# Two linear-attention and two MLP layers on one core: layer-norm statistics of the next layer's first four row tiles, dealt to two engines and issued later

## The chip, the core and the metric

The kernel runs on one core of one Trainium2 chip. A core has five engines, each with an instruction queue of its own that is worked in order: TensorE (PE in the profile; its weight loads are PEld), VectorE (DVE), ScalarE (ACT), GpSimd (POOL) and SyncE (SP), which issues the DMAs here. TensorE writes its results to PSUM, from where VectorE and ScalarE fetch them. The metric is the device time of one execution in microseconds (us).

## What is computed

x has 2048 rows of 576 features, in bfloat16. Four layers follow one another: attention, MLP, attention, MLP, with the same weights in both rounds. Cut to what matters:

```
def _layernorm(x): return (x - mean(x)) / sqrt(var(x) + 1e-5)

def A(x):                                    # 32 heads of 18
    q, k, v = split(x @ wqkv)
    phi = lambda t: where(t > 0, t + 1, exp(t)) + 1e-6
    kv  = sum over rows of phi(k)^T v        # per head
    z   = sum over rows of phi(k)
    return (phi(q) @ kv) / (phi(q) . z + 1e-6)  @ wo

def B(x):                                    # F = 4608
    y = _layernorm(x)
    return gelu(y @ w1 + b1) @ w2 + b2

x = x + A(_layernorm(x)); x = x + B(_layernorm(x))
x = x + A(_layernorm(x)); x = x + B(_layernorm(x))
```

B normalizes its already normalized input once more; the kernel does both at once, with one variance and a changed epsilon.

## The kernel before, in words

Rows are worked in 16 row tiles of 128 and in 4 chunks of 4 row tiles. An attention layer (`layer_A`, li = 0 and li = 2) first makes keys and values and their sums over all rows, and then, in its output stage, goes through the row tiles t = 0 to 15 (the loop at L827). The MLP layer that follows (`LayerB`) needs the first chunk, row tiles 0 to 3, normalized and transposed in `yT` before its first matmul; the other chunks it loads and normalizes later, beside its own matmuls.

**The output stage, one pass t.** `wo_stage(t)` (L787) multiplies the scaled features `pq` with `kvwo` (ten matmuls of 288 columns, L792, into one of two PSUM tiles, `accA` and `accB` in turns) and calls `residual`, where VectorE adds the old row and writes the new one (L515); SyncE stores it to `x_d` (L522). Then come the query projections that are left (`q_proj`, L585, whose features ScalarE makes with L464 and L465 and VectorE with L472 and L476), and the scaling of the next chunk: `den_stage(c)` (L746) makes the denominators of chunk c on TensorE (L754) and their reciprocals on ScalarE as exp(-ln) (L758, L761; the name of the last is kept in `act_last["rden"]`); `quad_stage` (L767) spreads them on VectorE; `scale_stage(g, c)` (L775), five times a chunk, broadcasts them over the head rows by a 512-column matmul (L780), ScalarE copies the result out of PSUM (L782), and VectorE multiplies `pq` by it (L783). Passes 0, 4 and 8 hold three broadcasts, passes 1, 5 and 9 two and behind them the denominators of the chunk after next. The broadcasts, the denominators, the query projections and the transposes below share four PSUM buffers (`ps_h`, tag h).

**The layer norm of a row tile** goes through `LNPipe`. `feed` adds an item, and each `tick` moves every item by one step; a pass of the output stage has two ticks up to t = 9 and one from then on. An item's `hold` counts ticks that it lets pass. The steps: statistics; `ln_rstd` on GpSimd (L372); `ln_nmr` on GpSimd (L376); the normalized row into one of three `y_ring` tiles on GpSimd (L389, with a small copy, L399); the transposes on TensorE (L421), not before pass `tp_at`; and their copy into `yT` on ScalarE (L428). Statistics there are in two kinds. With `stats="act"` ScalarE goes over the row twice, for the mean (L333, Identity with an accumulated sum) and in the next tick for the squares (L340), and GpSimd makes the variance (L342). With `stats="dve"` VectorE does two `bn_stats` (L349, L350), a `bn_aggr` (L356) and a scalar step (L366); if the item has `after`, the two `bn_stats` are ordered behind the instruction that `after` names, for "sum" the last residual sum issued so far.

**What sets the order.** The program's order is a wish: a scheduler puts each engine's instructions in order when they are ready by its own reckoning, earlier issued ones first. TensorE's order in these stages is fixed by a chain (`pe`). `add_manual_dep(..., NOSYNC, ...)` adds an edge of order between two instructions of one engine's queue, without a semaphore.

**Rows.** The new rows, the old rows that are loaded ahead (four tiles, `prefetch_xo`) and the pairs of old rows of the first layer share a ring of nine buffers (`rows`, tag row). A row of tiles 0 to 3 is held until it is stored and normalized.

Of the kernel before, what the change touches and what calls it, by code (L numbers as in the profile page):

```python
# [7 lines left out]
ACT = mybir.ActivationFunctionType  # L8
# [6 lines left out]
S, D, F, H, DH = 2048, 576, 4608, 32, 18  # L15
# [19 lines left out]
def build(tc, A_x, A_wqkv, A_wo, B_w1, B_b1, B_w2, B_b2, out, dbg=None, n_layers=4):  # L35
    nc = tc.nc
    dbg = dbg or {}
    with ExitStack() as ctx:
# [80 lines left out]
        def row_tile(name):  # L119
            return rows.tile([P, D], F32, name=name, tag="row")  # L120
# [3 lines left out]
        NOSYNC = mybir.DependencyInfo(mybir.DependencyClass.NoSync, mybir.DependencyReason.SCHED_ONLY)  # L124
# [13 lines left out]
        def pe(inst):  # L138
            if pe_chain["on"]:
                if pe_chain["last"] is not None:  # L140
                    tc.add_manual_dep(inst.ins, pe_chain["last"], NOSYNC, reason="TensorE order in the MLP")
                pe_chain["last"] = inst.ins.name
            return inst
# [157 lines left out]
        class LNPipe:  # L301
# [11 lines left out]
            def tick(self, transposes=1):  # L313
                land()
                for it in list(self.items):
# [8 lines left out]
                    if st == -1:  # L324
                        xn = row_tile("xl")
# [4 lines left out]
                    elif st == 0 and it["stats"] == "act":  # L330
                        mv = it["mv"] = work.tile([P, 2], F32, name="ln_mv", bufs=6)
                        it["dump"] = blk.tile([P, D], BF16, name="ln_dump", tag="blk")
                        nc.scalar.activation(out=it["dump"][:], in_=it["xt"][:, 0:D], func=ACT.Identity,  # L333
                                             scale=-1.0 / D, accum_out=mv[:, 0:1])
                        it["stage"] = 0.5
                        continue
                    elif st == 0.5:
                        u = it["u"] = work.tile([P, 1], F32, name="ln_u", bufs=4)
                        mv = it["mv"]
# [6 lines left out]
                    elif st == 0:  # L346
                        xt = it["xt"]
                        stt = work.tile([P, 2, 6], F32, name="ln_st", bufs=4)
                        first = nc.vector.bn_stats(out=stt[:, 0, :], in_=xt[:, 0:HALF])  # L349
                        second = nc.vector.bn_stats(out=stt[:, 1, :], in_=xt[:, HALF:D])  # L350
                        after = dve_last["sum"] if it["after"] == "sum" else it["after"]
# [3 lines left out]
                        mv = work.tile([P, 2], F32, name="ln_mv", bufs=6)  # L355
# [23 lines left out]
                    elif st in (2, 3):  # L379
# [4 lines left out]
                        xt = it["xt"]  # L384
                        if it["norm"] == "act":
                            nc.scalar.activation(out=y[:, 0:D], in_=xt[:, 0:D], func=ACT.Identity,
                                                 scale=it["rstd"][:, 0:1], bias=it["nmr"][:, 0:1])
# [18 lines left out]
                    elif st == 4:  # L406
                        y = it["y"]
                        t = it["t"]
# [6 lines left out]
                        first = it["kind"] == "A" and t < 2  # L415
# [26 lines left out]
        lnp = LNPipe()  # L442
        act_last = dict(exp=None, gelu=None)
# [57 lines left out]
        def residual(li, t, halves):  # L501
            xo = xo_of.pop((li, t))
            last = (li == n_layers - 1)
            if last:
                xn = rows.tile([P, 2 * D], BF16, name="xbf", tag="row")[:, 0:D]
            elif li == 0:
                xn = row_tile("xn")[:]
            else:
                xn = xo
            parts = [slice(h * HALF, (h + 1) * HALF) for h in range(2)] if last and t == NT - 1 else [slice(0, D)]  # L510
            for i, cols in enumerate(parts):
                if len(parts) == 2:
                    total = nc.vector.tensor_tensor(out=xn[:, cols], in0=halves[i][:, 0:HALF], in1=xo[:, cols], op=ALU.add)
                else:
                    total = nc.vector.tensor_tensor(out=xn[:, cols].rearrange("p (h n) -> p h n", h=2), in0=halves,  # L515
                                                    in1=xo[:, cols].rearrange("p (h n) -> p h n", h=2), op=ALU.add)
                dve_last["sum"] = total.ins.name
                if last:
                    nc.sync.dma_start(out=out_f[t * P:(t + 1) * P, cols], in_=xn[:, cols])
            if last:  # L520
                return None
            nc.sync.dma_start(out=x_d[t], in_=xn)  # L522
            return xn

        def layer_A(li, next_kind, pre_a1=None):
# [261 lines left out]
            def wo_stage(t):  # L787
                c, j = divmod(t, TPC)
                wp = ps_acc.tile([P, 2, 512], F32, name="wo_ps", tag=("accA", "accB")[t % 2])
                for half in range(2):  # L790
                    for g in range(G):
                        pe(nc.tensor.matmul(wp[:, half, 0:HALF], lhsT=pq[(g, c)][0:GR[g], j * P:(j + 1) * P],  # L792
                                              rhs=kvwo[g][0:GR[g], half * HALF:(half + 1) * HALF],
                                              start=(g == 0), stop=(g == G - 1)))
                xn = residual(li, t, wp[:, :, 0:HALF])
                if xn is not None and next_kind == "B" and t < TPC:
                    lnp.feed(xn, t, "B", "pool", "act", hold=1, stats="act", tp_at=6 + 2 * t)

            for t in range(AHEAD):
                prefetch_xo(li, t, add_b2=False)  # L800
# [26 lines left out]
            for t in range(NT):  # L827
                c, j = divmod(t, TPC)
                if t + AHEAD < NT:
                    prefetch_xo(li, t + AHEAD, add_b2=False)  # L830
                wo_stage(t)
                for late in list(rden_of):
                    quad_stage(late, after=dve_last["sum"])
                if q_left:
                    q_proj(*q_left.pop(0))
                if c + 1 < NCA:
                    for g in ((0, 1, 2), (3, 4), (), ())[j]:
                        scale_stage(g, c + 1)
                if j == 1 and c + 2 < NCA:
                    den_stage(c + 2)  # L840
                if t == NT - 3:
                    warm_table(ACT.Gelu_apprx_tanh, act_last["copy"])
                state["wo"] = t
                lnp.tick()
                if t < 10:
                    lnp.tick(transposes=0)
# [237 lines left out]
```

## Time and profile before

| | |
|---|---|
| median of 3 runs | 768.49 us (768.37 to 768.53) |
| the profiled execution, its own time | 768.48 us |
| its span, from the first instruction to the last | 766.7 us |
| TensorE busy | 760.5 us (99%) |
| ScalarE busy | 341.5 us (45%) |
| VectorE busy | 269.5 us (35%) |
| GpSimd busy | 123.9 us (16%) |
| output stage of the first attention layer | about 78 to 107 us |
| output stage of the second | about 454 to 482 us |

Times in the views are microseconds from the start of the span. A timeline row has start, length, engine, line, operation, out<-in with the program's tile names, shapes and count; in brackets the idle time of the engine before it and who ended it. A row of groups has busy time and the mean of one in ns. Matmuls overlap one another, so a busy TensorE is not one at its pace: that is read from the starts. The line numbers are those of the code above.

### The profile page before, as it was taken

The numbers are of one execution on the slowest core, as the hardware profiler recorded it, in microseconds if no ns is written. First come the engines' busy times: TensorE is split into PE (matmuls) and PEld (weight loads), VectorE is DVE, ScalarE is ACT, GpSimd is POOL, SyncE is SP. The second block draws the span as 40 slices with busy tenths as digits, with TensorE's granted clock in tenths as the row PEclk, the third lists the DMA queues.
The fourth block names the chain that finished last, engine by engine and source line by source line (L and its number), as shares of the span: only waits on it lengthen the run. The fifth ranks groups of instructions, "written<-read, shape, count | busy, mean of one in ns | idle before, by whom it ended". The sixth has DMA issues, their size and how long they took to land.

```text
span 766.7 us, 15671 instructions
## 1 busy us (share of the span) xinstructions
PE 760.5 (99%) x6522; PEld 492.6 (64%) x6522; DVE 269.5 (35%) x669; ACT 341.5 (45%) x768; POOL 123.9 (16%) x202
## 2 busy tenths in 40 slices
PE   9999999999999999999999999999999999999998
PEld 6776664675477457646777767447745764674476
DVE  7786764035113603400455677600140032000000
ACT  5888956304710660164056578560065027205600
POOL 4681412012100301200110004300020011001000
PEclk9999999999999999999999999999999999999999
DMA  9992483016402721330246007530131033011000
GB/s 262 264 302 48 140 276 79 28 57 164 123 24 62 194 70 40 96 87 1 73 122 214 1 16 247 203 81 15 51 107 50 17 124 81 9 32 55 2 9 24
DMA packets 80289, 73.82 MB, mean 96 GB/s; under 512 B 36698, under 2 KB 64858, under 8 KB 80218
## 3 DMA queue, kind: packets, MB, share of 16 engines
q1 hardware_dynamic: 80218, 72.82, 32.3%
q8 instruction: 51, 0.84, 0.5%
q14 instruction: 20, 0.16, 0.1%
HBM read 48.03 MB, written 24.77 MB: 95 GB/s over the span
## 4 chain that ended last, share of the span: by engine, by line
PE 96%; ACT 3%; DVE 1%; issue 0%; DMA 0%; ACTq 0%
PE m_ps L965 36%; PE h_ps L907 20%; PE hp_ps L907 16%; PE q_ps L585 5%; PE wo_ps L792 3%; PE k_ps L537 3%; PE k_ps L608 3%; PE k_ps L625 2%; PE v_ps L558 1%; PE m_half L965 1%; PE v_ps L555 1%; ACT rden_bc L782 1%; PE tp L421 1%; ACT ln_dump L333 1%; PE kvacc L579 1%; PE k_tail L625 1%
## 5 line engine op out<-in xcount | busy, mean ns | idle before, releaser
L965 PE MATMUL m_ps<-w_sb,hT 128*128 128x288 bf16 x2232 | 274.8, 286 | 0.0
L965 PEld LDWEIGHTS <-hT 128*128 128x128 bf16 x2304 | 224.8, 98 | 59.8 <-issue 3.4
L907 PEld LDWEIGHTS <-w_sb 64*128 64x128 bf16 x2304 | 124.5, 94 | 136.4 <-issue 1.9
L907 PE MATMUL hp_ps<-yT,w_sb 64*128 64x512 bf16 x1152 | 178.0, 376 | 0.0
L907 PE MATMUL h_ps<-yT,w_sb 64*128 64x512 bf16 x1152 | 147.9, 376 | 0.0
L912 ACT COPY relay_sb<-relay_sb 128x1 f32<-128x1 f32 x144 | 28.6, 198 | 262.9 <-PE h_ps L907 220.0
L903 ACT ACTIVATE hT<-h_ps,b1T 128x512 bf16<-128x512 f32 x144 | 91.2, 684 | 43.8 <-PE h_ps L907 43.8
L372 POOL TENSOR_TENSOR ln_rstd<-ln_u,neg_half 128x1 f32<-128x1 f32 x64 | 36.2, 567 | 376.8 <-DVE ln_u L363 225.6
L903 ACT ACTIVATE hT<-hp_ps,b1T 128x512 bf16<-128x512 f32 x144 | 91.2, 693 | 0.0
L515 DVE TENSOR_TENSOR xbf<-m_ps,xo 128x576 bf16<-128x576 f32 x15 | 11.4, 758 | 214.5 <-PE m_ps L965 214.5
L515 DVE TENSOR_TENSOR xo<-m_ps,xo 128x576 f32<-128x576 f32 x16 | 12.1, 758 | 174.6 <-PE m_ps L965 174.6
L498 POOL TENSOR_TENSOR xo<-xo,b_bc 128x576 f32<-128x576 f32 x32 | 41.0, 1286 | 100.5 <-DMA xo<-x_d 63.6
L907 PE MATMUL h_ps<-yT,w_tail 64*128 64x512 bf16 x144 | 54.1, 376 | 0.0
L907 PE MATMUL hp_ps<-yT,w_tail 64*128 64x512 bf16 x144 | 54.1, 376 | 0.0
L585 PE MATMUL q_ps<-yT,wqkv_sb 128*126 128x512 bf16 (+1 forms) x200 | 49.8, 380 | 0.0
L792 PE MATMUL wo_ps<-kvwo,pq 126*128 126x288 bf16 (+1 forms) x320 | 43.4, 286 | 0.4
L907 PEld LDWEIGHTS <-w_tail 64*128 64x128 bf16 x288 | 27.1, 94 | 17.1
L792 PEld LDWEIGHTS <-pq 126*128 126x128 bf16 (+1 forms) x320 | 30.1, 97 | 10.7 <-DVE pq L783 0.9
L464 ACT ACTIVATE phi_e<-k_ps 128x288 bf16<-128x288 f32 x46 | 19.3, 419 | 38.7 <-PE k_ps L608 35.8
L585 PEld LDWEIGHTS <-wqkv_sb 128*126 128x126 bf16 (+1 forms) x200 | 24.9, 131 | 11.7 <-issue 0.4
L472 DVE TENSOR_SCALAR phi_e<-phi_e 128x288 bf16<-128x288 bf16 (+2 forms) x86 | 24.8, 288 | 19.9 <-ACT phi_e L464 19.2
L464 ACT ACTIVATE phi_e<-q_ps 126x512 bf16<-126x512 f32 (+1 forms) x40 | 23.9, 598 | 17.1 <-PE q_ps L585 16.8
(133 smaller groups left out, 665.4 us busy)
## 6 DMA issues: line engine op xcount, KB each, us to landing
xo<-x_d SPq DMA_DIRECT2D x48, 288.0 KB
x_d<-xo SPq DMA_DIRECT2D x32, 288.0 KB
xl<-x_d SPq DMA_DIRECT2D x24, 288.0 KB
y_d<-turned SPq DMA_DIRECT2D x40, 144.0 KB
w_sb<-in_B_w_dram SPq DMA_DIRECT2D x6, 864.0 KB
yT<-y_d SPq DMA_DIRECT2D x10, 512.0 KB
w_sb<-in_B_w_dram SPq DMA_DIRECT2D x9, 512.0 KB
x_d<-xn SPq DMA_DIRECT2D x16, 288.0 KB
```

Source lines behind the costliest of these rows:

```text
L372: nc.gpsimd.tensor_tensor(out=rstd[:], in0=it["u"][:], in1=neg_half[:], op=ALU.pow)
L464: exp = nc.scalar.activation(out=e_out, in_=ps_ap, func=ACT.Exp)
L472: low = nc.vector.tensor_scalar(out=e[0:rows, 0:n], in0=e[0:rows, 0:n], scalar1=1.0, scalar2=1e-6, op0=ALU.min, op1=ALU.add)
L498: nc.gpsimd.tensor_tensor(out=xo[:], in0=xo[:], in1=b2_bc[:], op=ALU.add)
L515: total = nc.vector.tensor_tensor(out=xn[:, cols].rearrange("p (h n) -> p h n", h=2), in0=halves, in1=xo[:, cols].rearrange("p (h n) -> p ...
L537: pe(nc.tensor.matmul(kp[:, 0:HALF], lhsT=yT[:, k, tok], rhs=wqkv_sb[:, k, D + half * HALF: D + (half + 1) * HALF], start=(k == 0), stop=( ...
L585: pe(nc.tensor.matmul(qp[0:GR[g], :], lhsT=wqkv_sb[:, k, GO[g]:GO[g] + GR[g]], rhs=yT[:, k, c * CA:(c + 1) * CA], start=(k == 0), stop=(k ...
L792: pe(nc.tensor.matmul(wp[:, half, 0:HALF], lhsT=pq[(g, c)][0:GR[g], j * P:(j + 1) * P], rhs=kvwo[g][0:GR[g], half * HALF:(half + 1) * HALF ...
L903: act_last["gelu"] = nc.scalar.activation(out=to, in_=ps, func=ACT.Gelu_apprx_tanh, bias=b1T[:, f:f + 1], scale=1.0).ins.name
L907: mm = pe(nc.tensor.matmul(dst[n], lhsT=wt, rhs=mv, start=(seen[n] == 0), stop=(seen[n] == 8)))
L912: relay = nc.scalar.copy(out=relay_sb[:, 1:2], in_=relay_sb[:, 0:1])
L965: pe(nc.tensor.matmul(acc[half][:, 0:HALF], lhsT=hT[f][:, j * P:(j + 1) * P], rhs=w2_sb[:, f, half * HALF:(half + 1) * HALF], start=(f == ...
```

## The change

Two edits. In `wo_stage` the items of the four row tiles get `hold` 2, 4, 6 and 8 in place of 1; tiles 0 and 2 keep their statistics on ScalarE and get `after="rden"`, tiles 1 and 3 have them on VectorE, with `after="sum"`. In `tick`, the mean of an item with `after="rden"` is ordered behind the last reciprocal that ScalarE was given. With two ticks a pass, tile 0's mean is issued in the pass of tile 1, tile 1's statistics in that of tile 3, tile 2's mean in that of tile 5 and tile 3's statistics in that of tile 7; `tp_at` stays.

```
                     elif st == 0 and it["stats"] == "act":
                         mv = it["mv"] = work.tile([P, 2], F32, name="ln_mv", bufs=6)
                         it["dump"] = blk.tile([P, D], BF16, name="ln_dump", tag="blk")
-                        nc.scalar.activation(out=it["dump"][:], in_=it["xt"][:, 0:D], func=ACT.Identity,
-                                             scale=-1.0 / D, accum_out=mv[:, 0:1])
+                        one = nc.scalar.activation(out=it["dump"][:], in_=it["xt"][:, 0:D], func=ACT.Identity,
+                                                   scale=-1.0 / D, accum_out=mv[:, 0:1])
+                        if it["after"] == "rden":
+                            tc.add_manual_dep(one.ins, act_last["rden"], NOSYNC, reason="denominators first")
...
                 xn = residual(li, t, wp[:, :, 0:HALF])
                 if xn is not None and next_kind == "B" and t < TPC:
-                    lnp.feed(xn, t, "B", "pool", "act", hold=1, stats="act", tp_at=6 + 2 * t)
+                    lnp.feed(xn, t, "B", "pool", "act", hold=(2, 4, 6, 8)[t], tp_at=6 + 2 * t,
+                             **(dict(after="sum") if t % 2 else dict(stats="act", after="rden")))
```

## The prediction

> **What bounds the kernel now.** I read the page first, then TensorE's waits, then the timelines of the two stages that the change touches.
>
> ```profile
> span 766.7 us, 15671 instructions
> PE 96%; ACT 3%; DVE 1%; issue 0%; DMA 0%; ACTq 0%
> PE rden_ps L780 <- ACT rden_bc L782: 0.9, 2, 0.5
> ```
>
> TensorE is the bound: it has 96% of the chain that ended last, so only what it idles can be won. Its one wait of note behind the start is L780 on ScalarE's copies (L782), twice: once in each attention layer's output stage ("first", 78 to 107 us, and "second", 454 to 482). The first stage in two halves (columns: length; busy us and count of PE, PEld, DVE, ACT, POOL; granted clock; DMA):
>
> ```profile
> 78.00:92.30 14.30, 13.63 (x108) 8.49 (x109) 10.75 (x25) 14.16 (x36) 4.97 (x12) 1.00 0.40 132
> 92.30:107.40 15.10, 15.10 (x147) 11.59 (x149) 11.08 (x20) 9.13 (x18) 4.19 (x9) 1.00 0.73 249
> ```
>
> In the early half ScalarE is full (14.16 of 14.30 us) and TensorE is not; in the late half it is the other way round. The granted clock is 1.00. Now TensorE where it stalls (start, length, instruction), behind two rows that give its pace:
>
> ```profile
> 76.06 1.08 PE q_ps L585 x5
> 103.69 3.70 PE wo_ps L792 x30
> ...
> 83.28 0.59 PE L780 MATMUL rden_ps<-quad_rden,head_bc 128*128 128x512 bf16 x2
> 83.80 0.47 PE L754 MATMUL den_ps<-pq,zsel 127*32 127x128 bf16 x20
> ...
> 88.99 0.81 PE L780 MATMUL rden_ps<-quad_rden,head_bc 128*128 128x512 bf16 x3
> 89.75 1.39 PE L792 MATMUL wo_ps<-kvwo,pq 126*128 126x288 bf16 x10
> 90.98 0.38 PE L780 MATMUL rden_ps<-quad_rden,head_bc 128*128 128x512 bf16 x1
> 91.79 0.38 PE L780 MATMUL rden_ps<-quad_rden,head_bc 128*128 128x512 bf16 x1 [0.43 <-ACT rden_bc L782]
> 92.28 0.47 PE L754 MATMUL den_ps<-pq,zsel 127*32 127x128 bf16 x20
> ...
> 459.50 4.11 PE L792 MATMUL wo_ps<-kvwo,pq 126*128 126x288 bf16 x30
> 463.45 0.81 PE L780 MATMUL rden_ps<-quad_rden,head_bc 128*128 128x512 bf16 x3
> ...
> 465.34 0.38 PE L780 MATMUL rden_ps<-quad_rden,head_bc 128*128 128x512 bf16 x1
> 466.17 0.38 PE L780 MATMUL rden_ps<-quad_rden,head_bc 128*128 128x512 bf16 x1 [0.46 <-ACT rden_bc L782]
> 466.66 0.47 PE L754 MATMUL den_ps<-pq,zsel 127*32 127x128 bf16 x20
> ```
>
> A 512-column matmul takes 1.08 / 5 = 0.216 us of the stream; thirty of L792, three row tiles, take 3.70. So the fifth broadcast of a chunk starts 0.81 - 0.22 = 0.59 us late in the first stage and 0.83 - 0.22 = 0.61 in the second. The denominators (L754) behind it follow 0.27 late in both; but where nothing waits (83.28 to 83.80, two broadcasts) that switch costs 0.52 - 0.43 = 0.09 anyway, so 0.18 is stall. In the second stage thirty L792 take 463.45 - 459.50 = 3.95, which is 0.25 too long. In the first the row tile at 89.75 starts 0.76 - 0.65 = 0.11 late.
>
> Why it stalls: four PSUM buffers (tag h) hold the broadcasts, so the fifth needs the first one's copy. ScalarE's queue there:
>
> ```profile
> 83.58 0.63 ACT L464 ACTIVATE phi_e<-q_ps 126x512 bf16<-126x512 f32 x1
> ...
> 90.42 0.76 ACT L340 ACTIVATE ln_dump<-xn,ln_mv 128x576 bf16<-128x576 f32 x1
> ...
> 91.18 1.53 ACT L782 CAST rden_bc<-rden_ps 126x512 bf16<-126x512 f32 x3
> ...
> 459.29 0.71 ACT L333 ACTIVATE ln_dump<-xo 128x576 bf16<-128x576 f32 x1
> ...
> 459.97 1.08 ACT L782 CAST rden_bc<-rden_ps 126x512 bf16<-126x512 f32 x2
> 460.91 0.30 ACT L758 ACTIVATE den_ps<-den_ps 128x128 f32<-128x128 f32 x1
> ...
> 465.53 1.56 ACT L782 CAST rden_bc<-rden_ps 126x512 bf16<-126x512 f32 x3
> ```
>
> The first broadcast is written at 88.99 + 0.38 = 89.37 but copied at 91.18, 1.81 us later, behind means and squares; in the second stage it is 463.83 and 465.53. At 459.29 a mean stands ahead of two copies by 0.68; the multiplies that need them, and the sum of tile 2 that stands behind these on VectorE, are late by as much, and TensorE wants that sum's PSUM bank for tile 4: the 0.25.
>
> **The change, part by part.**
>
> *Tiles 0 and 2 stay on ScalarE, later.* A mean holds the queue for 0.68 us, a square for 0.76 (distances of starts above): 1.44 a tile. With hold=2 tile 0's mean is issued in the pass of tile 1, and its order edge puts it behind chunk 2's reciprocal (L758, L761). First stage, with every length at its most: the q pass of tile 1 from 83.58 takes 2 x 0.63, two copies 1.08, Ln and Exp 2 x 0.30, mean and square 1.44, the q pass of tile 2 1.26: 89.2. The broadcasts come at 89.37, and ScalarE is free. Second stage: copies from 459.29 take 1.08, the reciprocal 0.60, mean and square 1.44: 462.4, against 463.83. The first copy then lands about 0.6 later, at 90.0 and 464.4, ahead of TensorE's need at 91.2 and 465.3. Both pairs of stalls go: 0.59 + 0.18 + 0.61 + 0.18 = **1.56**. The mean at 459.29 moves off too: **0.25**. Tile 2's pair comes behind chunk 3's reciprocal, in the half where ScalarE idles 15.10 - 9.13 = 6 us: nothing.
>
> *Tiles 1 and 3 go to VectorE.* ScalarE loses 1.44 us a tile, GpSimd its L342. VectorE gets:
>
> ```profile
> L349 DVE BATCH_NORM_STATS2 ln_st<-xo 128x6 f32<-128x288 f32 x16 | 6.9, 430 | 0.1
> L356 DVE BATCH_NORM_AGGREGATE ln_mv<-ln_st 128x2 f32<-128x12 f32 x56 | 11.3, 202 | 1.3
> L366 DVE TENSOR_SCALAR ln_u<-ln_mv 128x1 f32<-128x1 f32 x24 | 3.5, 147 | 0.6
> L515 DVE TENSOR_TENSOR xn<-wo_ps,xo_pair 128x576 f32<-128x576 f32 x16 | 12.0, 753 | 3.5 <-PE wo_ps L792 3.5
> ```
>
> Two statistics (L349, L350), one aggregate, one scalar: 0.43 x 2 + 0.20 + 0.15 = 1.21 us a tile. VectorE has 14.30 - 10.75 = 3.5 us idle in the early half and 4.0 in the late one. The order edges are on one queue each, with no wait on another engine: tile 1's stand behind the sum of tile 3, tile 3's behind that of tile 7. Queued behind them is the next tile's sum, and TensorE waits for that one's bank. In the first stage the sum of tile 3 ends at 89.7 (TensorE starts on its bank at 89.75); the sum of tile 4 could then end at 89.7 + 1.2 + 0.75 = 91.7, and tile 6 wants its bank behind the denominators, which now start at 92.28 - 0.77 = 91.5 and last some 0.4. Cover of 0.2, the thinnest of all. I take nothing; bounds 0 and 0.2 lost.
>
> *The 0.11 at 89.75* comes from the sum of tile 3, behind the q pass of tile 2, which ends about where it did. I take nothing; bounds 0 and 0.11 won.
>
> *What is late next.* GpSimd normalizes the tiles later, and TensorE's transposes of them keep their places (tp_at):
>
> ```profile
> 103.25 0.44 PE L421 MATMUL tp<-ident,y_ring 128*128 128x128 bf16 x5
> ...
> 467.50 0.72 POOL L372 TENSOR_TENSOR ln_rstd<-ln_u,neg_half 128x1 f32<-128x1 f32 x1
> ...
> 469.82 0.64 POOL L399 COPY y_ring<-y_ring 128x64 bf16<-128x64 bf16 x1
> ```
>
> From 467.50 to 470.46 GpSimd needs 3.0 us a tile, the slow case. Tile 3 is last: sum of tile 7 near 95.5, statistics 96.7, normalized 99.7; its transpose stands at 103.25 - 0.8 = 102.4. Cover of 2.7 us.
>
> **Sum:** 1.56 + 0.25 = 1.81 us, against the profiled execution's own 768.48 (span 766.7 and 1.8 around it; the median of the runs shown is 768.49, the same): 768.48 - 1.81 = **766.7**. All stalls found make 1.92 and 766.6.
>
> **Rivals.**
>
> (a) *VectorE beside GpSimd*, 767.4:
>
> ```profile
> 86.91 1.08 POOL L389 TENSOR_SCALAR y_ring<-xn,ln_rstd,ln_nmr 128x576 bf16<-128x576 f32 x1
> ...
> 87.43 0.84 DVE L767 TENSOR_TENSOR quad_rden<-quad_mask,rden 128x512 bf16<-128x512 bf16 x1
> ...
> 88.61 0.42 DVE L476 TENSOR_TENSOR pq<-phi_a,phi_e 72x512 bf16<-72x512 bf16 x1
> L767 DVE TENSOR_TENSOR quad_rden<-quad_mask,rden 128x512 bf16<-128x512 bf16 x8 | 3.8, 474 | 2.4 <-ACT rden L761 2.2
> ```
>
> Beside a normalization L767 took 0.84, against a mean of 0.47. The change moves tile 0's normalization from 86.91 to about 89, next to L476 at 88.61. Should it start first, L476 waits up to 0.8, and with it the sum of tile 3, on which TensorE already waits at 89.75: some 0.7 lost, 766.7 + 0.7 = 767.4. For it: the two are 0.4 us apart. Against: L476 goes first by my times. [...]
>
> (b) *Rows held longer*, 767.7, and in full **slower**, 768.9. A tile's row of the nine-buffer ring is read until the tile is normalized. That rows wait for this already shows in SyncE's waits:
>
> ```profile
> SPq L493 <- POOL y_ring L389: 3.3, 2, 2.4
> 94.20 2.63 PE L792 MATMUL wo_ps<-kvwo,pq 126*128 126x288 bf16 x20
> 97.60 1.40 PE L792 MATMUL wo_ps<-kvwo,pq 126*128 126x288 bf16 x10
> ```
>
> In the first stage chunk 3's reciprocal now ends near 93.0 and tile 2's mean and square near 94.5; 3.0 us of GpSimd less its last copy free the row at 97.1. If the sum of tile 7 (ready at 94.20 - 0.77 + 1.4 = 94.8) takes that row, it ends at 97.8, and tile 9, due on its bank at 97.60 - 0.77 = 96.8, is 1.0 late: 767.7. Tile 3's statistics, behind that sum, then free its row at about 101.5; if the sum of tile 9 takes it, tile 11, due at 103.25 - 2.47 - 0.77 + 1.0 = 101.0, is 1.2 late: 768.9. It turns slower once both waits pass 1.81. Against: the rows of tiles 4 and 5 come free earlier, with their stores.
>
> (c) *The change does not act*, 768.5: a scheduler orders the queues, and the copies could stand behind other work. Against: the edge is explicit, and in the second stage ScalarE has 463.83 - 462.4 = 1.4 us to spare.
>
> **Chances.** Forecast 0.56; (a) 0.12; (b) 0.10 at 767.7 and 0.14 in full, half of it beyond 770.0, since the ring's rows are the one resource that I cannot follow row by row; (c) 0.08. A measurement of this kernel can tell 0.2%, 1.5 us, from no change: faster is below 766.95, slower above 770.0. So faster 0.56, slower 0.07, within 0.37. The range 766.4 to 768.5 holds the forecast with its bounds of 0.11 won and 0.2 lost, (a), the milder (b) and half of (c): 0.82. The likeliest case alone is 766.5 to 766.9.
>
> **What would show it.** Right: L780's wait on L782 is gone from TensorE's waits, the fifth broadcast follows the fourth by 0.22, no L333 stands between two L782 of one chunk, and the stages end 0.8 and 1.8 us earlier. (a) shows as an L476 of 0.8 us before the sum of tile 3; (b) as a VectorE sum that waits for GpSimd, or a SyncE load that waits longer; (c) as L780 still waiting. All of it would be wrong if the statistics, moved behind one chunk's reciprocal, met the next chunk's copies.

## The result and the profile after

| | before | after |
|---|---|---|
| median of 16 runs each | 768.44 us (767.83 to 768.67) | 766.96 us (766.62 to 767.25) |
| ratio after to before, 95% interval | | 0.9981 (0.9974 to 0.9989) |
| the profiled execution, its own time | 768.48 us | 767.19 us |
| its span | 766.7 us | 765.4 us |

The changed kernel is 1.48 us faster by the medians, 0.19%: the direction of the forecast, 0.26 us above its 766.7 and inside its range, but 0.06 above its likeliest case (766.5 to 766.9) and just inside the 0.2% that were called no change. The clock granted is 1.00 in both.

In the code after, lines behind L333 stand 2 further down (L780 is L782, the copies L782 are L784, the multiplies L783 are L785, `wo_stage`'s matmuls L794, the sum L517), the MLP's first matmul is L910 for L907. The page of the kernel after, its line on the chain that ended last:

```profile
PE 97%; ACT 1%; DVE 1%; DMA 1%; POOL 0%; issue 0%; SPq 0%; DVEq 0%
```

ScalarE's share of the chain falls from 3% to 1%. The waits of TensorE and of VectorE, kernel after (sum in us, times, longest):

```profile
PE wo_ps L794 <- DVE xn L517: 0.4, 1, 0.4
DVE xn L517 <- POOL y_ring L391: 1.1, 1, 1.1
```

The wait of the broadcasts (L782) on ScalarE's copies (L784) is gone, both times. Two rows are new in these stages: once TensorE waits for a residual sum, and once such a sum waits for GpSimd. Where in time it changed is read from the two output stages. I measure a stage from its first `wo_ps` matmul to the first `h_ps` matmul of the MLP, since what lies ahead of the first stage differs from run to run by up to a microsecond (the last section). The four ends in TensorE's timeline, of the kernel before:

```profile
77.68 0.67 PE L792 MATMUL wo_ps<-kvwo,pq 126*128 126x288 bf16 x4
...
107.32 0.82 PE L907 MATMUL h_ps<-yT,w_sb 64*128 64x512 bf16 x6
...
454.07 0.67 PE L792 MATMUL wo_ps<-kvwo,pq 126*128 126x288 bf16 x4
...
481.70 0.60 PE L907 MATMUL h_ps<-yT,w_sb 64*128 64x512 bf16 x4
```

and of the kernel after:

```profile
77.72 0.67 PE L794 MATMUL wo_ps<-kvwo,pq 126*128 126x288 bf16 x4
...
107.02 1.04 PE L910 MATMUL h_ps<-yT,w_sb 64*128 64x512 bf16 x8
...
453.77 1.10 PE L794 MATMUL wo_ps<-kvwo,pq 126*128 126x288 bf16 x5
...
480.37 1.04 PE L910 MATMUL h_ps<-yT,w_sb 64*128 64x512 bf16 x8
```

The first stage goes from 29.64 to 29.30 us, 0.34 won; the second from 27.64 (481.70 - 454.07, rounded) to 26.60, 1.04 won. The stretch between them is 346.75 in both. So 1.38 us come from the two stages; the spans differ by 1.3, and what lies outside the stages differs by less than 0.1. The first stage ends 0.30 us earlier and the second 1.33, where the prediction gave 0.8 and 1.8 as the signs of being right. The forecast had 0.77 for the first and 1.04 for the second: the second came out within a hundredth, and 0.43 is missing in the first. The first stage's halves, as shown of before, in the kernel after:

```profile
78.00:92.30 14.30, 14.16 (x129) 9.19 (x127) 12.03 (x31) 12.46 (x30) 3.26 (x6) 1.00 0.43 142
92.30:107.10 14.80, 14.42 (x125) 10.93 (x125) 10.88 (x22) 8.63 (x18) 6.17 (x13) 1.00 0.72 244
```

In the early half TensorE's busy time rises from 13.63 to 14.16 of 14.30 and ScalarE's falls from 14.16 to 12.46. But the late half, which TensorE filled before, now has 14.80 - 14.42 = 0.38 idle. The timeline of TensorE, kernel after, shows both:

```profile
89.03 0.81 PE L782 MATMUL rden_ps<-quad_rden,head_bc 128*128 128x512 bf16 x3
89.68 1.40 PE L794 MATMUL wo_ps<-kvwo,pq 126*128 126x288 bf16 x10
90.91 0.60 PE L782 MATMUL rden_ps<-quad_rden,head_bc 128*128 128x512 bf16 x2
91.44 0.47 PE L756 MATMUL den_ps<-pq,zsel 127*32 127x128 bf16 x20
91.83 1.41 PE L794 MATMUL wo_ps<-kvwo,pq 126*128 126x288 bf16 x10
...
93.36 1.40 PE L794 MATMUL wo_ps<-kvwo,pq 126*128 126x288 bf16 x10
95.14 1.39 PE L794 MATMUL wo_ps<-kvwo,pq 126*128 126x288 bf16 x10 [0.38 <-DVE xn L517]
...
459.21 3.87 PE L794 MATMUL wo_ps<-kvwo,pq 126*128 126x288 bf16 x30
462.92 0.81 PE L782 MATMUL rden_ps<-quad_rden,head_bc 128*128 128x512 bf16 x3
...
464.81 0.59 PE L782 MATMUL rden_ps<-quad_rden,head_bc 128*128 128x512 bf16 x2
465.33 0.47 PE L756 MATMUL den_ps<-pq,zsel 127*32 127x128 bf16 x20
```

The fourth and fifth broadcasts are one row now ("x2", 0.60 and 0.59 long), and the denominators follow 0.53 and 0.52 behind them, the 0.52 of a place without a stall. Thirty L794 take 462.92 - 459.21 = 3.71 where they took 3.95. The row tile at 89.68 follows its broadcasts by 0.65, not 0.76. New is the last row of the first part: ten matmuls of a row tile take 3.71 / 3 = 1.24, so tile 8 could start at 93.36 + 1.24 = 94.60 and starts at 95.14, **0.54 us late**. It waits for the sum of tile 6, which has to clear its PSUM tile.

VectorE and GpSimd around that sum, kernel after, VectorE first:

```profile
90.03 0.74 DVE L517 TENSOR_TENSOR xn<-wo_ps,xo_pair 128x576 f32<-128x576 f32 x1
...
91.09 0.14 DVE L368 TENSOR_SCALAR ln_u<-ln_mv 128x1 f32<-128x1 f32 x1
91.16 0.75 DVE L785 TENSOR_TENSOR pq<-pq,rden_bc 126x512 bf16<-126x512 bf16 x2
...
92.49 0.75 DVE L785 TENSOR_TENSOR pq<-pq,rden_bc 126x512 bf16<-126x512 bf16 x2
94.33 0.76 DVE L517 TENSOR_TENSOR xn<-wo_ps,xo_pair 128x576 f32<-128x576 f32 x1 [1.09 <-POOL y_ring L391]
...
91.33 0.99 POOL L374 TENSOR_TENSOR ln_rstd<-ln_u,neg_half 128x1 f32<-128x1 f32 x1 [0.95 <-DVE ln_u L368]
92.42 0.95 POOL L378 TENSOR_SCALAR ln_nmr<-ln_mv,ln_rstd 128x1 f32<-128x1 f32 x1
93.47 0.82 POOL L391 TENSOR_SCALAR y_ring<-xn,ln_rstd,ln_nmr 128x576 bf16<-128x576 f32 x1
```

The matmuls that the sum of tile 6 reads end at 91.83 + 1.41 = 93.24, but it starts at 94.33, as soon as L391, the normalization of **tile 1**, has read its row (93.47 + 0.82 = 94.29). That it is the row, and not a queue, is what the experiments have to show. Two things make tile 1 late. Its two `bn_stats` stand behind the sum of tile 3, and its aggregate and scalar step (L368) behind the sum of tile 4, so GpSimd gets them at 91.23. And two steps on a single column, L374 and L378, take 0.99 and 0.95 us beside VectorE's multiplies, where the same steps of tile 2 take 0.55 and 0.26 (94.95 and 95.61). With those lengths L391 would end near 93.2, about when the sum of tile 6 is ready. Only the first attention layer can lose this way: there `residual` takes a new row of the ring for every sum, while in the second it writes the sum over the old row (`xn = xo`).

### The profile page after: what moved, and what is told of

Its sections match the earlier page's. It is cut to its first block, busy times and chain, and to the rows that moved or that the text cites. A ratio compares the mean times of both kernels' runs of the same rounds, so it can differ in the third digit from the quotient of the medians.

```text
span 765.4 us, 15654 instructions
## 1 busy us (share of the span) xinstructions
PE 759.5 (99%) x6522; PEld 492.3 (64%) x6522; DVE 271.8 (36%) x685; ACT 336.9 (44%) x752; POOL 123.4 (16%) x198
## 4 chain that ended last, share of the span: by engine, by line
PE 97%; ACT 1%; DVE 1%; DMA 1%; POOL 0%; issue 0%; SPq 0%; DVEq 0%
PE m_ps L968 36%; PE h_ps L910 20%; PE hp_ps L910 16%; PE q_ps L587 5%; PE wo_ps L794 4%; PE k_ps L539 3%; PE k_ps L610 3%; PE k_ps L627 2%; PE v_ps L560 1%; PE m_half L968 1%; PE v_ps L557 1%; PE tp L423 1%; PE rden_ps L782 1%; DMA wqkv_sb<-in_A_wqkv_dram 1%; PE kvacc L581 1%; PE k_tail L627 1%
## 5 line engine op out<-in xcount | busy, mean ns | idle before, releaser
L910 PEld LDWEIGHTS <-w_sb 64*128 64x128 bf16 x2304 | 124.5, 94 | 136.5 <-issue 1.9
L910 PE MATMUL hp_ps<-yT,w_sb 64*128 64x512 bf16 x1152 | 178.0, 376 | 0.0
L910 PE MATMUL h_ps<-yT,w_sb 64*128 64x512 bf16 x1152 | 148.0, 376 | 0.0
L374 POOL TENSOR_TENSOR ln_rstd<-ln_u,neg_half 128x1 f32<-128x1 f32 x64 | 36.7, 575 | 375.0 <-DVE ln_u L365 226.8
L517 DVE TENSOR_TENSOR xbf<-m_ps,xo 128x576 bf16<-128x576 f32 x15 | 11.4, 758 | 212.8 <-PE m_ps L968 212.8
L517 DVE TENSOR_TENSOR xo<-m_ps,xo 128x576 f32<-128x576 f32 x16 | 12.1, 758 | 174.5 <-PE m_ps L968 174.5
L910 PE MATMUL h_ps<-yT,w_tail 64*128 64x512 bf16 x144 | 54.1, 376 | 0.0
L910 PE MATMUL hp_ps<-yT,w_tail 64*128 64x512 bf16 x144 | 54.1, 376 | 0.0
L794 PE MATMUL wo_ps<-kvwo,pq 126*128 126x288 bf16 (+1 forms) x320 | 43.4, 286 | 0.7 <-DVE xn L517 0.4
L910 PEld LDWEIGHTS <-w_tail 64*128 64x128 bf16 x288 | 27.1, 94 | 17.1
L794 PEld LDWEIGHTS <-pq 126*128 126x128 bf16 (+1 forms) x320 | 30.1, 97 | 10.9 <-DVE pq L785 0.9
```

The costliest lines, as they stand in the source:

```text
L374: nc.gpsimd.tensor_tensor(out=rstd[:], in0=it["u"][:], in1=neg_half[:], op=ALU.pow)
L910: mm = pe(nc.tensor.matmul(dst[n], lhsT=wt, rhs=mv, start=(seen[n] == 0), stop=(seen[n] == 8)))
```

## The experiments

**Theories.** *Row*: the sum of tile 6 writes its result into tile 1's row of the ring, and waits until GpSimd has read it; the 0.54 lost goes with any edit that gives the sum another row or frees this one earlier. *Order of the statistics*: the loss comes from the order of VectorE's queue or from VectorE's load, and then remains when only the row changes. And on the gain, *order* (means put behind the reciprocals) against *load* (ScalarE relieved of two tiles).

All times in one table; the stage lengths are taken as above, and the ratio is to the kernel before on the same chip (768.17 us, 30 runs, for row_out, tile1_early, hold_only and split_only; 768.47, 31 runs, for the others).

| kernel | first stage | second stage | median, us | ratio, 95% interval |
|---|---|---|---|---|
| before | 29.64 | 27.64 | | |
| after, run again (changed_again) | 29.30 | 26.60 | 766.97 | 0.9981 (0.9971 to 0.9990) |
| row_out | 28.76 | 26.60 | 766.23 | 0.9974 (0.9964 to 0.9984) |
| tile1_early | 28.75 | 26.60 | 766.41 | 0.9977 (0.9968 to 0.9986) |
| hold_only | 28.75 | 26.60 | 766.50 | 0.9978 (0.9969 to 0.9987) |
| tile1_later | 28.76 | 26.75 | 766.52 | 0.9977 (0.9968 to 0.9986) |
| split_only | 28.75 | 27.04 | 766.71 | 0.9981 (0.9972 to 0.9990) |
| psum_mult | 29.47 | 26.60 | 767.02 | 0.9982 (0.9973 to 0.9992) |
| before_row_out | 29.63 | 27.63 | 768.22 | 0.9995 (0.9985 to 1.0004) |

The intervals of the medians of the changed kernels overlap; the stage lengths, which agree within 0.01 us in the two profiles of the kernel after, tell the kernels apart (one profile for each of the others).

**changed_again**: no edit.

> The changed kernel once more, beside the others on one chip: first stage 29.30, second 26.60, with GpSimd's two stretched steps in it again, if they are a matter of order and not of chance.

Measured: both stages and both stretched GpSimd steps as before, within 0.01 us. The new stall belongs to the order of the kernel, not to chance.

**row_out**: the new row of tile 1 in the first attention layer goes into a tile that is free at that time, outside the ring; all else as in the kernel after.

```
+            elif li == 0 and t == 1:
+                xn = turned[:].rearrange("p a b c -> p (a b c)").bitcast(F32)[:, 0:D]
             elif li == 0:
```

> The changed kernel, with the new row of tile 1 of the first layer kept in another buffer than the ring's nine; orders and statistics as changed. Theory (row): the changed kernel loses 0.55 us ahead of tile 8 in the first stage because the sum of tile 6 takes tile 1's row and waits for its normalization. Then VectorE's wait for L391 goes, TensorE's gap ahead of tile 8 goes, and the time is 0.5 us below the changed kernel's 766.96: about 766.4. GpSimd's two stretched steps (0.99 and 0.95 us) stay. Rival (VectorE's load): the added statistics make the sums late; the gap stays, 767.0.

Measured: first stage 28.76, the 0.54 is back. The sum of tile 6 (now L519, with GpSimd below it), kernel row_out:

```profile
92.28 0.76 DVE L519 TENSOR_TENSOR xn<-wo_ps,xo_pair 128x576 f32<-128x576 f32 x1
...
90.33 0.99 POOL L374 TENSOR_TENSOR ln_rstd<-ln_u,neg_half 128x1 f32<-128x1 f32 x1 [0.94 <-DVE ln_u L368]
91.44 0.95 POOL L378 TENSOR_SCALAR ln_nmr<-ln_mv,ln_rstd 128x1 f32<-128x1 f32 x1
92.48 0.83 POOL L391 TENSOR_SCALAR y_ring<-turned,ln_rstd,ln_nmr 128x576 bf16<-128x576 f32 x1
```

This run is 1.00 us earlier by its start. GpSimd is as slow as before, step for step, and the sum no longer waits for it: it starts 0.20 us *ahead* of the normalization. So the wait was for the row. *Order of the statistics* falls: VectorE's queue is the same.

**before_row_out**: the same edit on the kernel before.

> The kernel before, with tile 1's row of the first layer outside the ring: a control. Theory (row): before, no sum waited for a normalization, so the row is worth nothing there: first stage 29.64, time as before. Rival (a ring that is one row larger helps in itself): first stage 0.3 us shorter or more.

Measured: 29.63 and 27.63, as before within 0.01; the two waits on ScalarE's copies are there. The row costs nothing while the statistics come early, so row_out's gain is no gain of its own. Its median stands 0.25 us under the kernel before's with equal stages, which is how far medians here can be trusted.

**tile1_early**: tile 1's statistics two ticks earlier.

```
-hold=(2, 4, 6, 8)[t]
+hold=(2, 2, 6, 8)[t]
```

> The changed kernel with hold 2, 2, 6, 8: tile 1's statistics one pass earlier, still on VectorE. Theory (row): tile 1's row is free about 2 us earlier, before the sum of tile 6 wants it: the gap ahead of tile 8 goes, about 766.4, unless the earlier statistics hold up the sum of tile 3 or 4 (each 0.1 late costs 0.1). Rival (VectorE's load): as much work on VectorE, so about 767.0, the gap at another tile.

Measured: 28.75. GpSimd's L374 and L378 and the sum of tile 6, kernel tile1_early:

```profile
89.36 0.55 POOL L374 TENSOR_TENSOR ln_rstd<-ln_u,neg_half 128x1 f32<-128x1 f32 x1
...
90.08 0.43 POOL L378 TENSOR_SCALAR ln_nmr<-ln_mv,ln_rstd 128x1 f32<-128x1 f32 x1
...
92.64 0.76 DVE L517 TENSOR_TENSOR xn<-wo_ps,xo_pair 128x576 f32<-128x576 f32 x1 [0.49 <-PE wo_ps L794]
```

The row is free before the sum is due (L391 ends at 90.61 + 0.87 = 91.48), and the sum waits for TensorE, as it should.

**tile1_later**: tile 1's statistics two ticks later.

```
-hold=(2, 4, 6, 8)[t]
+hold=(2, 6, 6, 8)[t]
```

> The changed kernel with hold 2, 6, 6, 8: tile 1's statistics one pass later (behind the sum of tile 4). Theory (row): if the sum of tile 6 still takes tile 1's row, it waits about 1 us longer than in the changed kernel, and the first stage grows from 29.30 to about 30.3 us, above the 29.64 of before. If the scheduler gives it another row, the wait moves to a later sum or goes, and the stage is 28.75. Rival (VectorE's load): the same work, 29.3.

Measured: not the longer stage, but 28.76, and no sum that waits for GpSimd. The sum of tile 6 and the normalization of tile 1, kernel tile1_later:

```profile
93.10 0.76 DVE L517 TENSOR_TENSOR xn<-wo_ps,xo_pair 128x576 f32<-128x576 f32 x1
...
93.60 0.82 POOL L391 TENSOR_SCALAR y_ring<-xn,ln_rstd,ln_nmr 128x576 bf16<-128x576 f32 x1
```

The sum starts half a microsecond ahead of the normalization, so it must have another row: held longer, tile 1's was no longer the one that the ring gave it (the views don't name the rows). The wait is thus not "the later, the longer": it hangs on who is given the row. (The second stage has 0.15 us more than in the kernel after, near its end; the cause stays open.)

**psum_mult**: in the first attention layer chunk 2's five multiplies read the broadcast in PSUM, without ScalarE's copy, so that they have one input in SBUF in place of two.

```
+                if li == 0 and c == 2:
+                    mult = nc.vector.tensor_tensor(out=pq[(g, c)][0:GR[g], 0:CA], in0=pq[(g, c)][0:GR[g], 0:CA],
+                                                   in1=bp[0:GR[g], 0:CA], op=ALU.mult)
+                    dve_last["mult"] = mult.ins.name
+                    return
```

> The changed kernel, but in the first layer the five multiplies of chunk 2 (L783 before) read the broadcast from PSUM, with no copy on ScalarE: one SBUF input instead of two. Theory (GpSimd's two steps for tile 1, 0.99 and 0.95 us, are stretched by multiplies with two SBUF inputs): the steps come back to about 0.55 and 0.27, tile 1's row is free by 93.2 and the gap ahead of tile 8 goes, first stage 28.8 us, if the longer multiplies (some 0.65 us by the row of the sums, which read PSUM too) do not hold up a sum. Rival (they are stretched by something else, such as the sums or the copies): 0.9 and more stay, first stage 29.3 us.

Measured: VectorE's multiplies (L784 here) and GpSimd beside them, kernel psum_mult:

```profile
90.81 1.27 DVE L784 TENSOR_TENSOR pq<-pq,rden_ps 126x512 bf16<-126x512 bf16 x2
...
90.97 0.55 POOL L374 TENSOR_TENSOR ln_rstd<-ln_u,neg_half 128x1 f32<-128x1 f32 x1 [1.21 <-DVE ln_u L368]
91.63 0.26 POOL L378 TENSOR_SCALAR ln_nmr<-ln_mv,ln_rstd 128x1 f32<-128x1 f32 x1
92.00 0.82 POOL L391 TENSOR_SCALAR y_ring<-xn,ln_rstd,ln_nmr 128x576 bf16<-128x576 f32 x1
```

GpSimd's two steps are back at 0.55 and 0.26 although VectorE multiplies all along. The edit takes away ScalarE's five copies as well, but these are not it: in the kernel after the copies end at 92.40, before L378 starts at 92.42, and in tile1_early L374 takes 0.55 (89.36) beside copies (88.75 to 90.31). Nor is it the sums: in the kernel before L372 takes 0.55 (89.48) beside two of them (88.95 to 90.36). What is left is the multiplies with both inputs in SBUF. With the second input in PSUM its type changes as well, f32 for bf16, and each multiply takes longer (below); which of the three counts was not taken apart. Nor is a step held by as much beside each of them: in the second stage of the kernel after, L374 takes only 0.65 beside two such multiplies (464.83), and why it lost 0.44 in the first stage is not shown. Tile 1's row is read at 92.82, ahead of the sum of tile 6. The stage is 29.47 all the same, for a reason of the edit's own: a multiply from PSUM takes 0.63 us (90.20) in place of 0.37 (90.81 in the kernel after), and it keeps the broadcast's buffer for that long. TensorE's fifth broadcast, in that kernel:

```profile
90.30 0.38 PE L782 MATMUL rden_ps<-quad_rden,head_bc 128*128 128x512 bf16 x1
90.88 0.38 PE L782 MATMUL rden_ps<-quad_rden,head_bc 128*128 128x512 bf16 x1 [0.20 <-DVE ln_u L368]
91.54 0.47 PE L756 MATMUL den_ps<-pq,zsel 127*32 127x128 bf16 x20 [0.28 <-POOL ln_rstd L374]
```

It follows the fourth by 0.58, and the denominators follow it by 0.66: 1.24 together, where a place without a stall has 0.52, which is the 0.72 that this stage is longer than hold_only's. (The releasers named there are what ended last by the profile; by the code the buffers wait for the multiplies, which VectorE works at that time.)

**hold_only**: all four tiles stay on ScalarE, with the change's holds and behind the reciprocals.

```
-                             **(dict(after="sum") if t % 2 else dict(stats="act", after="rden")))
+                             stats="act", after="rden")
```

> Only the second half of the change: all four statistics stay on ScalarE, with hold 2, 4, 6, 8 and behind the reciprocals. Theory (order, not load, made the stalls of before): the copies of a chunk meet at most one mean and square, ScalarE has the room for 1.44 us between two chunks, and tile 1's row is free by 93: all stalls go, about 766.5. Rival (ScalarE's load): four tiles are 5.7 us too many in the early half, and one stall pair of 0.6 to 0.8 a stage stays: 767.3 to 768.

Measured: 28.75 and 26.60. *Order* holds and *load* falls: ScalarE keeps all its work, later, and every stall goes. (The holds and the edge were not tried one without the other.) Its queue at chunk 2, kernel hold_only:

```profile
88.43 0.68 ACT L333 ACTIVATE ln_dump<-xn 128x576 bf16<-128x576 f32 x1
...
89.23 0.78 ACT L342 ACTIVATE ln_dump<-xn,ln_mv 128x576 bf16<-128x576 f32 x1
...
90.00 2.50 ACT L784 CAST rden_bc<-rden_ps 126x512 bf16<-126x512 f32 x5
```

One mean and one square stand ahead of the copies, from 88.43 on, where two means and two squares stood from 88.21 on in the kernel before; the first copy starts at 90.00 in place of 91.18, and its buffer is free when the fifth broadcast wants it. The change's second part, the move of tiles 1 and 3 to VectorE, isn't needed here, and with it (and tile 1's hold of 4) comes the new stall.

**split_only**: the other part alone: tiles 1 and 3 on VectorE, holds of 1, no edge behind the reciprocals.

```
-hold=(2, 4, 6, 8)[t], tp_at=6 + 2 * t,
-                             **(dict(after="sum") if t % 2 else dict(stats="act", after="rden")))
+hold=1, tp_at=6 + 2 * t,
+                             **(dict(after="sum") if t % 2 else dict(stats="act")))
```

> Only the first half of the change: tiles 1 and 3 on VectorE behind the sums, hold 1 as before and no edge behind the reciprocals. Theory (order): the mean of tile 0 stays ahead of two copies in the second stage (0.25 us stays), the mean and square of tile 2 stay ahead of chunk 2's copies but alone; 0.2 to 0.6 of each pair of stalls may stay: 766.9 to 767.6. Rival (load): with 2.9 us less on ScalarE a stage the pairs go whole: 766.8 and only the 0.25 is left.

Measured: 28.75 in the first stage, 27.04 in the second, 0.44 more than in the kernel after. TensorE, VectorE and ScalarE in the second, kernel split_only:

```profile
458.11 2.64 PE L794 MATMUL wo_ps<-kvwo,pq 126*128 126x288 bf16 x20
461.03 1.14 PE L794 MATMUL wo_ps<-kvwo,pq 126*128 126x288 bf16 x8 [0.27 <-DVE ln_u L368]
...
458.77 0.45 DVE L351 BATCH_NORM_STATS2 ln_st<-xo 128x6 f32<-128x288 f32 x1
...
457.90 0.71 ACT L333 ACTIVATE ln_dump<-xo 128x576 bf16<-128x576 f32 x1
...
458.58 1.08 ACT L784 CAST rden_bc<-rden_ps 126x512 bf16<-126x512 f32 x2
```

Tile 0's mean stands ahead of two copies, as in the kernel before, and tile 1's two statistics (the second, L352, at 459.14) stand ahead of two multiplies (459.50) and of the sum of tile 2 behind these (460.27 to 460.97), for which TensorE's bank waits (the row names L368, which ended last); tile 4 starts 461.03 - (458.11 + 2 x 1.24) = 0.44 late, where it was 0.25 in the kernel before. How much of the 0.44 each of the two makes was not taken apart. So splitting alone is enough in the first stage, not in the second; the holds and the edge are enough in both.

## Why the prediction was right, and where it was not

- **Both pairs of stalls**, 1.56 (0.77 and 0.79): right, to 0.01 each (TensorE's timeline after). The copies of chunk 2 start at 89.44 in the first stage and 463.34 in the second, straight behind the broadcasts; these are rows of ScalarE, kernel after:

```profile
89.44 1.56 ACT L784 CAST rden_bc<-rden_ps 126x512 bf16<-126x512 f32 x3 [0.90 <-PE rden_ps L782]
...
457.58 2.52 ACT L784 CAST rden_bc<-rden_ps 126x512 bf16<-126x512 f32 x5
...
463.34 1.56 ACT L784 CAST rden_bc<-rden_ps 126x512 bf16<-126x512 f32 x3 [1.21 <-PE rden_ps L782]
```

  ScalarE idles 0.90 and 1.21 us ahead of them; the prediction had worked out that it would be free in time with every length at its most.
- **The 0.25** of the second stage: right; the five copies at 457.58 are one row, with no mean among them, and thirty L794 take 3.71.
- **The 0.11 at 89.75, taken as nothing**: wrong in size, it was won. The sum of tile 3 stands ahead of tile 2's last query multiply now (L517 at 88.31, L478 at 88.97), and behind it before (L476 at 88.61, L515 at 88.95). The first stage shows it in row_out: 29.64 - 28.76 = 0.88 = 0.59 + 0.18 + 0.11. All stalls found, 1.92 us, do go where nothing new comes: row_out's stages are 0.88 + 1.04 = 1.92 us shorter (its medians differ by 768.17 - 766.23 = 1.94).
- **Statistics on VectorE, nothing**: right for what it spoke of. The sum of tile 4 stands behind them and ends at 90.03 + 0.74 = 90.77; TensorE wants the bank at 91.83. I had feared 91.7, since I let the sum of tile 3 end at 89.7 (it ends at 89.06) and put the aggregate and the scalar step ahead of the sum of tile 4 as well; the scheduler put only the two statistics there.
- **The step that failed** is the sum itself: it held no term for rows held longer. That stood in the prediction as rival (b), with the sign by which it would show ("a VectorE sum that waits for GpSimd"), and this sign is what came; but I put it on tile 2's row and the sum of tile 7, with 1.0 us. It came on tile 1's row and the sum of tile 6, with 0.54. My walk through the ring followed the rows of tiles 2 and 3 and left out that tile 1's statistics, behind the sum of tile 3, are late as well. That the forecast came within 0.26 us all the same is in part luck: the uncounted 0.11 and 0.10 between medians and stages made up for some of the 0.54.
- **Rival (a)**, VectorE beside GpSimd: the slowing came, but on the other side. No L478 was stretched (0.41 at 88.97 in the kernel after); GpSimd's two small steps were, by (0.99 - 0.55) + (0.95 - 0.26) = 1.13 us, and that made tile 1 late enough for the row to matter. That L478 went first, as the prediction said, was close: it started 0.07 us ahead of tile 0's normalization (L391 at 89.04, which took 1.04). (a) and (b) were put as alternatives; here the one fed the other.
- **(c)**: the change acts. **Tile 3's transpose**, with a cover of 2.7 us: no row of TensorE's waits names a transpose.

In numbers: 1.81 forecast + 0.11 not counted - 0.54 for the row = 1.38, the sum of the two stages. The medians, 1.48, lie 0.10 away, less than the 0.25 of the control.

## What to carry to other kernels

Where a late step reads a buffer of a ring, moving it later keeps the buffer: walk the ring and ask for each moved reader who writes next into what it reads, and who waits for that writer. Before work is dealt to another engine, try its order alone; here four later issue times and an edge did all, and with the dealing came the one loss. And when a wait is found, undo what it is thought to wait for and leave its lateness as it is (row_out): only that tells the dependency from the delay.

## What the runs showed of the hardware

In the two output stages of the kernel after, GpSimd's steps on one column (128x1) take 0.55 us (L374, four of eight) and 0.26 or 0.27 (L378, seven of eight). The two of tile 1 in the first stage take 0.99 (91.33) and 0.95 (92.42) beside VectorE multiplies with both inputs in SBUF (91.16 to 91.91 and 92.49 to 93.24; between them VectorE works a sum). In psum_mult, beside the same multiplies with one input in PSUM, they take 0.55 and 0.26 (90.97 and 91.63). I had not expected that an operation of 128 numbers could lose more than its own length, 0.69 us on 0.26. The price isn't fixed: beside two such multiplies L374 took 0.99 and 0.65 in the kernel after (91.33 and 464.83) and 0.70 in hold_only (90.73), and beside the first of three in tile1_early (89.36) it kept its 0.55.

The time ahead of the first stage varies by 1.00 us among these profiles (76.72 in row_out, 77.72 in the kernel after). TensorE's wait for the first weights differs too (none in the kernel before, 0.6 in the kernel after, 1.1 in hold_only), but doesn't follow that time run by run, and its cause stays open. Differences of half a microsecond are therefore read from stage lengths here, not from spans.
